# A decode step on one Trainium2 core: V's products at 256 columns, one quarter of wo in uneven loads, x in one load

## The chip, the cores and the metric

The kernel runs on one core of one Trainium2 chip. A core has a matrix engine (TensorE, PE in the profile; its weight loads are PEld), a vector engine (DVE), a scalar engine (ACT), a general engine (POOL), and SyncE (SP), which here only issues DMAs. Sixteen DMA engines bring data from HBM into SBUF, the on-chip memory of 128 partitions; PE writes its sums to PSUM. The metric is the device time of one execution in microseconds, the median of several runs. Times in the profile and in the trace are counted from the start of the profiled span.

## The reference

For 8 sequences of one new token each, the input x (8 x 512) is layer-normed to xn. Two branches use xn, and their product is added to x:

```python
q = (xn @ wq)                       # 32 heads of 128; 8 KV heads, so 4 query heads share one
k, v = last 1024 rows of the caches # of 4096, for each sequence and KV head
p = softmax(q k^T / sqrt(128))
s = (p v) @ wo                      # 4096 -> 512
g = silu((gelu(xn @ w_gate) * (xn @ w_up)) @ w_down)   # 512 -> 1792 -> 512
out = x + s * g
```

All inputs are bf16. Read in a run: K and V windows of 8 sequences (16 MB each in units of 1,048,576 bytes), wq and wo (4 MB each), and the three feed-forward matrices (1.75 MB each), 47.46 million bytes in all.

## The kernel before, in words

The order of the work is written out by hand: each engine runs its instructions in the order of the program, and waits are put in between by the framework, for data and for buffers.

All large loads go through SP's queue, in this order: the first quarter of wo (`wo_first`, line 106), wq (line 109), K of sequence 0, K of 1, V of 0 (line 84, each cache block in two loads of 1 MB, one for each half `g` of the KV heads), then K and V of the following sequences alternating, w_gate and w_up (line 438), w_down (line 441), and the other three quarters of wo (line 451). The buffers are a ring of eight slots of 2 MB. The compiled program has eight completion semaphores for all loads together, x's included; a load is issued when the load eight places before it has landed and when its buffer is free. A load of 128 partitions consists of one packet for each contiguous row: 8 KB for K, V and a quarter of wo, 32 KB for wq, 14 KB for the feed-forward matrices. The last quarter of wo comes in three pieces (5, 2 and 1 KB for each partition), so that products can start on the first of them. x comes through ACT's queue, in five loads of 2, 2, 2, 1 and 1 rows (line 79).

Ahead of the loop over the sequences: DVE takes the mean and variance of x (line 145), ACT the root (line 149), DVE scales (`xhat`, line 152), and ACT loads its table for the exponential by a small activation into a tile of its own (`warm`, line 162). PE multiplies xn with wq (line 261), and the queries are laid out block-diagonally (`qbd`).

For each sequence `b` the functions below run in an order that overlaps sequences:

- `turn_k` transposes one half of K on DVE (line 249), `scores` makes the products with the queries (line 311).
- `softmax` takes the maximum (lines 321 to 328), and ACT forms the exponentials and, through its accumulator, their sums over the row (line 333). The sums go to a column of the tile `sums`.
- `turn_p` transposes the probabilities on DVE (line 344). `values` multiplies them with V (line 355): for each of the two halves `g`, 32 products of 128 columns, in four column groups of PE that accumulate side by side.
- `keep_o` copies the result to SBUF on ACT (line 368); `gather` adds the four groups up on PE with a selection matrix, first the 128 values (line 376), and then the sums (line 380), once for each `g`. `regroup` divides by the sums and turns the result for wo, once for four sequences.

After the loop come the products with w_gate and w_up (line 465), the gelu, those with w_down (line 494), and at last the 128 products with wo (line 513) in the order of its quarters. Two DVE steps (lines 521 and 523) and one output DMA (line 525) end the kernel.

Of the kernel before, what the change touches and what calls it, by code (L numbers as in the profile page):

```python
# [7 lines left out]
ACT = mybir.ActivationFunctionType  # L8
# [3 lines left out]
FP32 = mybir.dt.float32  # L12
# [9 lines left out]
def kernel(  # L22
# [13 lines left out]
    nc = tc.nc  # L36

    B, Sq, D = A_x.shape
    Hkv, Sk, Dh = A_k_cache.shape[1], A_k_cache.shape[2], A_k_cache.shape[3]
# [6 lines left out]
    P = nc.NUM_PARTITIONS  # L46
    NK = D // P
    HG = 4
    NG = Hkv // HG
    C = W * HG // P  # L50
# [7 lines left out]
    keep = ctx.enter_context(tc.tile_pool(name="keep", bufs=1))  # L58
    two = ctx.enter_context(tc.tile_pool(name="two", bufs=2))
# [7 lines left out]
    def slot(name):  # L67
        i = taken[0] % N_SLOTS
        taken[0] += 1
        if i >= 2:  # L70
            return ring.tile([P, 2 * ROW], BF16, name=name, tag="slot")
        if not late:
            late.append(ctx.enter_context(tc.tile_pool(name="late", bufs=2)))
        return late[0].tile([P, 2 * ROW], BF16, name=name, tag="slot")


    x_sb = keep.tile([B, D], BF16, name="x_sb")
    for r, z in ((0, 2), (2, 4), (4, 6), (6, 7), (7, 8)):
        nc.scalar.dma_start(out=x_sb[r:z], in_=A_x.flatten_outer_dims()[r:z])  # L79

    def load_cache(cache, b, name):
# [10 lines left out]
    k_sb, v_sb = {}, {}  # L92
# [4 lines left out]
    def load_v(b):  # L97
# [3 lines left out]
    wo_src = [  # L101
        A_wo[u * 1024 : (u + 1) * 1024, :].rearrange("(p j) d -> p j d", j=8)
        for u in range(NU)
    ]
# [14 lines left out]
        out=ident,  # L119
        in_=ident,  # L120
# [13 lines left out]
        out=xpad,  # L134
        in_=xpad,
# [8 lines left out]
    stats = keep.tile([B, nc.vector.BN_STATS_DIM], FP32, name="stats")  # L144
# [3 lines left out]
    rstd = keep.tile([B, 1], FP32, name="rstd")  # L148
# [4 lines left out]
        out=xhat,  # L153
# [4 lines left out]
        op1=ALU.mult,  # L158
    )
    x_res = keep.tile([P, DT], FP32, name="x_res")  # L160
    warm = keep.tile([B, 1], FP32, name="warm")
    nc.scalar.activation(out=warm, in_=rstd, func=ACT.Exp)  # L162
    with tc.tile_pool(name="ps_x", bufs=1, space=PSUM) as ps_x:
        xnT_ps = ps_x.tile([P, NK, B], BF16, name="xnT_ps")
        xv = xhat.rearrange("b (p k) -> b k p", k=NK)
# [5 lines left out]
        for t in range(4):  # L171
# [4 lines left out]
                start=True,  # L176
                stop=True,
# [12 lines left out]
        out=hv,  # L190
        in_=hv,
# [7 lines left out]
        out=neg_st,  # L199
        in_=neg_st,  # L200
# [8 lines left out]
        out=neg_mv,  # L209
        in_=neg_mv,  # L210
# [9 lines left out]
    sel = consts.tile([P, NG, Hq], FP32, name="sel")  # L220
    nc.vector.memset(sel, 0.0)
    for g in range(NG):
        nc.vector.tensor_reduce(
            out=sel[:, g, g * qd : (g + 1) * qd],
            in_=ident.rearrange("p (t g h) -> p g h t", t=4, g=NG)[:, g],
# [5 lines left out]
        out=own, in_=ident.rearrange("p (i e) -> p e i", e=8), axis=AX.X, op=ALU.add  # L231
    )
    pick = consts.tile([P, 4 * NU], BF16, name="pick")
    with nc.allow_low_precision(reason="sums of zeros and a single one"):
        nc.vector.tensor_reduce(
            out=pick, in_=ident.rearrange("p (a e) -> p a e", e=8), axis=AX.X, op=ALU.add
# [20 lines left out]
    with tc.tile_pool(name="ps_q", bufs=1, space=PSUM) as ps_q:  # L257
        q_ps = [ps_q.tile([P, 512], FP32, name=f"q_ps{i}") for i in range(8)]
        for k in range(NK):
            for i in range(8):  # L260
# [4 lines left out]
                    start=(k == 0),  # L265
                    stop=(k == NK - 1),
                )
        for half in range(2):
            for i in range(4 * half, 4 * half + 4):
                e = nc.vector.tensor_copy if i % 4 == 3 else nc.scalar.copy  # L270
# [7 lines left out]
    for j in range(4):  # L278
        sl = slice(32 * j, 32 * j + 32)
        for m in range(2):  # L280
            for g in range(NG):
                e = nc.scalar.copy if (4 * j + 2 * m + g) % 3 == 2 else nc.vector.tensor_copy
# [3 lines left out]


    pT, S, P_sb, O_ps = {}, {}, {}, {}
    sums = keep.tile([P, B], FP32, name="sums")

    actx = ExitStack()
    ps_s = actx.enter_context(tc.tile_pool(name="ps_s", bufs=2, space=PSUM))
# [26 lines left out]
    def softmax(b):  # L319
        mx = two.tile([P, 1], FP32, name="mx")  # L320
        nc.vector.tensor_reduce(  # L321
            out=mx, in_=S[b].rearrange("p a c -> p (a c)"), axis=AX.X, op=ALU.max
        )

        m2 = two.tile([64, 1], FP32, name="m2")
        nc.vector.tensor_tensor(out=m2, in0=mx[0:64, :], in1=mx[64:128, :], op=ALU.max)
        m1 = two.tile([32, 1], FP32, name="m1")
        nc.vector.tensor_tensor(out=m1, in0=m2[0:32, :], in1=m2[32:64, :], op=ALU.max)  # L328
        nb = two.tile([P, 1], FP32, name="nb")
        for j in range(4):  # L330
            nc.scalar.mul(nb[32 * j : 32 * j + 32, :], m1, -inv)  # L331
        P_sb[b] = two.tile([P, C // 2, 32, 2], BF16, name="P_sb")
        nc.scalar.activation(  # L333
            out=P_sb[b].rearrange("p c i w -> p c w i"),
            in_=S[b].rearrange("p a (c w i) -> p (a c) w i", w=2, i=32),
            func=ACT.Exp,
            bias=nb,
            scale=inv,
            accum_out=sums[:, b : b + 1],
        )  # L340

    def turn_p(b):
        pT[b] = two.tile([P, C // 2, Hq, 2], BF16, name="pT")
        nc.vector.transpose(  # L344
            out=pT[b].rearrange("p c h w -> p (c h w)").bitcast(I32),
            in_=P_sb[b].rearrange("p c i w -> p (c i w)").bitcast(I32),
        )

    def values(b):
        O_ps[b] = ps_o.tile([P, NG, Dh], FP32, name="O_ps")  # L350
        for g in range(NG):
            vv = v_sb[b][:, g].rearrange("p (c d) -> p c d", d=Dh)
            for c in range(C):
                t = c % 4
                nc.tensor.matmul(  # L355
                    O_ps[b][32 * t : 32 * t + 32, g, :],
                    pT[b][:, c // 2, :, c % 2],
                    vv[:, c, :],
                    start=(c < 4),
                    stop=(c >= C - 4),  # L360
                )

    o_ps = {}
    O_sb = {}

    def keep_o(b):
        O_sb[b] = two.tile([P, NG, Dh], FP32, name="O_sb")
        nc.scalar.copy(out=O_sb[b], in_=O_ps[b])  # L368

    def gather(b):  # L370
        q = b % 4
        if q == 0:
            o_ps[b // 4] = ps_g.tile([P, Dh + 1], FP32, name="o_ps")
        o = o_ps[b // 4][32 * q : 32 * q + 32, :]
        for g in range(NG):
            nc.tensor.matmul(  # L376
                o[:, 0:Dh], sel[:, g, :], O_sb[b][:, g, :], start=(g == 0), stop=(g == NG - 1)
            )
        for g in range(NG):
            nc.tensor.matmul(  # L380
                o[:, Dh : Dh + 1],
                sel[:, g, :],
                sums[:, b : b + 1],
                start=(g == 0),
                stop=(g == NG - 1),
            )

    def regroup(q):

# [24 lines left out]
    for b in range(B):  # L414
        if b + 2 < B:
            load_k(b + 2)
        if b + 1 < B:
            load_v(b + 1)
            turn_k(b + 1, 0)
        softmax(b)  # L420
        if b + 1 < B:
            scores(b + 1, 0)
        if b >= 1:
            gather(b - 1)
        if b + 1 < B:
            turn_k(b + 1, 1)
            scores(b + 1, 1)
        turn_p(b)
        values(b)
        keep_o(b)  # L430
        if b == 4:
            regroup(0)
# [10 lines left out]
    for u in range(1, NU):  # L443
        if u % 2 == 1:
            pair = slot("wo_sb").rearrange("p (v j d) -> p v j d", v=2, d=D)
        t = pair[:, (u - 1) % 2]
        pieces = [(0, 8)]
        if u == NU - 1:
            pieces = [(0, 5), (5, 7), (7, 8)]
        for a, z in pieces:  # L450
            nc.sync.dma_start(out=t[:, a:z, :], in_=wo_src[u][:, a:z, :])
        wo.append(t)

    gather(B - 1)
    regroup(1)
    actx.close()
# [4 lines left out]
    for n, ws in (("z_ps", wgu[0]), ("u_ps", wgu[1])):  # L461
        ps = ps_f.tile([P, FT], FP32, name=n)
        for k in range(NK):
            for t in range(4):
# [4 lines left out]
                    start=(k == 0),  # L469
                    stop=(k == NK - 1),  # L470
# [6 lines left out]
        out=z2, in0=z2, scalar1=0.044715, scalar2=1.0, op0=ALU.mult, op1=ALU.add  # L477
# [11 lines left out]
        out=hT.rearrange("p j b -> p (j b)"), in_=h_bf.rearrange("p (y j) -> p j y", j=NJ)  # L489
    )  # L490
    f_ps = ps_f.tile([P, DT], FP32, name="f_ps")
    for j in range(NJ):
        for t in range(4):
# [4 lines left out]
                start=(j == 0),  # L498
                stop=(j == NJ - 1),
# [4 lines left out]
        out=g_sb, in0=g_sb, scalar1=0.5, scalar2=0.5, op0=ALU.mult, op1=ALU.add  # L504
# [5 lines left out]
    for u in range(NU):  # L510
        for j in range(8):
            for t in range(4):
# [4 lines left out]
                    start=(u == 0 and j == 0),  # L517
                    stop=(u == NU - 1 and j == 7),
# [7 lines left out]
        out=out_f.rearrange("b (t d) -> t b d", t=4), in_=out_sb[0 : P : RB, :]  # L526
# [31 lines left out]
```

## Time and profile before

| | |
|---|---|
| median of 3 runs | 120.89 us (120.85 to 120.97) |
| the profiled execution | 120.88 us |
| its span | 119.0 us |
| busy PE / DVE / ACT | 72.0 / 75.8 / 31.4 us |
| PE records (matmuls; as many weight loads) | 992 |
| DMA moved | 47.60 MB, mean 400 GB/s |
| V products (line 355) | 512, 9.5 us |
| gather of the values (line 376) | 32 records, 5.4 us |
| O_sb copies on ACT (line 368) | 8, 372 ns each |

The strip of slices gives, for 40 equal parts of the span, the busy share of each engine in tenths, the share of the DMA engines and what they moved. The list of DMA queues tells whose packets they were: q1 is SP's, q10 is ACT's, q8 and q14 carry instructions to the engines. The chain of work that ended last is followed back from the last instruction, at each step to what released it. A group is all instructions of one line, engine and shape, with the idle time of the engine ahead of them and what ended it. Busy time by stretch gives the same for chosen parts of the span, with the PE clock that was granted, the DMA share and GB/s at the end of a row. The trace holds besides, for each DMA packet, start, length, size and queue.

### The profile page before, as it was taken

The page shows a single profiled execution, that of the slowest core. Times are in us where ns is not written, and L with a number is a line of the kernel's source. Part 1 is how long each engine was busy: PE and PEld are TensorE (multiplying, and loading weights), DVE is VectorE, ACT ScalarE, POOL GpSimd, SP SyncE. Part 2 cuts the span into 40 slices and gives each one's busy share as a digit, 9 for nine tenths or more (in the row PEclk, how much of TensorE's full clock was granted, in tenths as well). Part 3 has the DMA queues.
Part 4 walks back from the last instruction along what each step waited for, and adds up shares of the span by engine and source line. Part 5 has one row for each costly group of instructions (what it writes and reads, how often), then busy time and mean ns, then how long its engine had stood idle before and what let it go on. Part 6 is the DMA issues. An engine that isn't in the chain of part 4 may idle for free.

```text
span 119.0 us, 2306 instructions
## 1 busy us (share of the span) xinstructions
PE 72.0 (61%) x992; PEld 37.5 (32%) x992; DVE 75.8 (64%) x101; ACT 31.4 (26%) x75; POOL 3.2 (3%) x10
## 2 busy tenths in 40 slices
PE   0000079941599596979964875698399264844650
PEld 0000033410133253545532434244135253414530
DVE  1000487999999999999957995971994224165100
ACT  1300230096202417170531421151070800120000
POOL 2000052000000000000000000000000000000000
PEclk9999999999679999999999999689859955578595
DMA  2998999999999999999999999999999999999930
GB/s 72 458 507 375 391 421 424 435 427 427 427 430 419 424 435 419 427 430 416 432 424 424 421 430 427 419 435 421 427 424 427 440 434 430 419 431 416 415 138 3
DMA packets 6109, 47.60 MB, mean 400 GB/s; under 512 B 716, under 2 KB 852, under 8 KB 1108
## 3 DMA queue, kind: packets, MB, share of 16 engines
q1 hardware_dynamic: 6084, 47.46, 94.6%
q8 instruction: 7, 0.11, 0.3%
q14 instruction: 2, 0.02, 0.0%
q10 hardware_dynamic: 16, 0.01, 0.0%
HBM read 47.46 MB, written 0.01 MB: 399 GB/s over the span
## 4 chain that ended last, share of the span: by engine, by line
DMA 61%; DVE 15%; PE 15%; ACT 3%; issue 2%; ACTq 1%; DVEq 0%
DMA wo_sb<-in_A_wo_dram 19%; DMA k_sb<-in_A_k_cache_dram 17%; DMA v_sb<-in_A_v_cache_dram 17%; DMA x_sb<-in_A_x_dram 9%; PE q_ps L261 7%; PE S_ps L311 6%; DVE kT L249 6%; DVE qbd L284 2%; DVE mx L321 2%; DVE q_both L274 1%; ACT P_sb L333 1%; ACTq L79 1%; ACT L162 1%; DVE q_both L271 1%; PE O_ps L355 1%
## 5 line engine op out<-in xcount | busy, mean ns | idle before, releaser
L311 PE MATMUL S_ps<-kT,qbd 128*128 128x512 bf16 x128 | 34.8, 420 | 15.4 <-DVE kT L249 12.0
L249 DVE STREAM_TRANSPOSE kT<-k_sb 128x2048 int32<-128x2048 int32 x16 | 36.6, 2289 | 5.0 <-DMA k_sb<-in_A_k_cache_dram 4.9
L311 PEld LDWEIGHTS <-qbd 128*128 128x128 bf16 x128 | 13.0, 103 | 33.3 <-issue 18.0
L331 ACT ACTIVATE nb<-m 32x1 f32<-32x1 f32 x32 | 6.4, 201 | 22.9 <-DVE m L328 22.6
L333 ACT ACTIVATE P_sb<-S_ps,nb 128x1024 bf16<-128x1024 f32 x8 | 11.1, 1391 | 0.3
L355 PE MATMUL O_ps<-v_sb,pT 128*32 128x128 bf16 x512 | 9.5, 231 | 2.6 <-DVE pT L344 2.6
L321 DVE TENSOR_REDUCE mx<-S_ps 128x1 f32<-128x1024 f32 x8 | 9.6, 1195 | 1.7 <-PE S_ps L311 1.6
L355 PEld LDWEIGHTS <-pT 128*32 128x32 bf16 x512 | 8.0, 103 | 5.6 <-issue 3.0
L261 PE MATMUL q_ps<-wq_sb,xnR 128*128 128x512 bf16 x32 | 9.2, 460 | 0.5 <-ACT x_res L179 0.5
L167 PE MATMUL xnT_ps<-ident,xhat 8*128 8x8 bf16 x4 | 0.3, 174 | 15.0 <-DVE xhat L152 15.0
L368 ACT COPY O_sb<-O_ps 128x256 f32<-128x256 f32 x8 | 3.0, 372 | 23.7 <-PE O_ps L355 23.7
L145 DVE BATCH_NORM_STATS2 stats<-x_sb 8x6 f32<-8x512 bf16 x1 | 0.7, 683 | 11.8 <-DMA x_sb<-in_A_x_dram 11.8
L344 DVE STREAM_TRANSPOSE pT<-P_sb 128x512 int32<-128x512 int32 x8 | 5.7, 711 | 3.4 <-ACT P_sb L333 3.3
L376 PE MATMUL o_ps<-O_sb,sel 128*32 128x128 f32 x32 | 5.4, 296 | 1.0 <-ACT O_sb L368 1.0
L300 PE MATMUL S_ps<-neg_mv,neg_st 128*128 128x512 bf16 x16 | 4.8, 381 | 1.9 <-DVE q_both L271 1.9
L261 PEld LDWEIGHTS <-xnR 128*128 128x128 bf16 x32 | 3.6, 114 | 5.8 <-issue 3.0
L271 ACT CAST q_both<-q_ps 128x512 bf16<-128x512 f32 x6 | 3.0, 613 | 7.9 <-PE q_ps L261 7.9
L167 PEld LDWEIGHTS <-xhat 8*128 8x128 bf16 x4 | 0.2, 114 | 15.0 <-DVE xhat L152 15.0
L376 PEld LDWEIGHTS o_ps<-O_sb,sel 128*32 128x32 f32 x32 | 3.0, 115 | 4.7 <-issue 3.2
L513 PE MATMUL s_ps<-wo_sb,oT 128*32 128x128 bf16 x96 | 2.7, 252 | 2.2 <-DMA wo_sb<-in_A_wo_dram 2.2
L252 DVE MEMSET qbd<- 128x4096 uint32 x1 | 3.5, 3472 | 0.8 <-issue 0.8
L513 PEld LDWEIGHTS <-oT 128*32 128x32 bf16 x128 | 3.0, 123 | 2.8 <-issue 2.6
(65 smaller groups left out, 51.1 us busy)
## 6 DMA issues: line engine op xcount, KB each, us to landing
k_sb<-in_A_k_cache_dram SPq DMA_DIRECT2D x16, 1024.0 KB, 19.7
v_sb<-in_A_v_cache_dram SPq DMA_DIRECT2D x16, 1024.0 KB, 19.8
wq_sb<-in_A_wq_dram SPq DMA_DIRECT2D x1, 4096.0 KB, 14.2
wo_sb<-in_A_wo_dram SPq DMA_DIRECT2D x2, 1024.0 KB
wgu_sb<-in_B_w_gate_dram SPq DMA_DIRECT2D x1, 1792.0 KB
wgu_sb<-in_B_w_up_dram SPq DMA_DIRECT2D x1, 1792.0 KB
wd_sb<-in_B_w_down_dram SPq DMA_DIRECT2D x1, 1792.0 KB, 25.1
wo_first<-in_A_wo_dram SPq DMA_DIRECT2D x1, 1024.0 KB, 4.8
```

Of the source, the lines that this page charges most:

```text
L249: nc.vector.transpose(out=t.bitcast(I32), in_=k_sb[b][:, g].bitcast(I32))
L261: nc.tensor.matmul(q_ps[i], xnR[:, k, :, :].rearrange("p j b -> p (j b)"), wq_sb[k][:, i * 512 : (i + 1) * 512], start=(k == 0), stop=(k = ...
L271: e(out=q_bf[:, i * 512 : (i + 1) * 512], in_=q_ps[i])
L300: nc.tensor.matmul(S[b][:, half, :], neg_st.rearrange("p j h -> p (j h)"), neg_mv.rearrange("p a n -> p (a n)"), start=True, stop=False,)
L311: nc.tensor.matmul(S[b][:, half, :], qbd[:, m, b, w, g, :], kv[:, half * 16 : (half + 1) * 16, m, :, w], start=False, stop=(g == NG - 1 an ...
L321: nc.vector.tensor_reduce(out=mx, in_=S[b].rearrange("p a c -> p (a c)"), axis=AX.X, op=ALU.max)
L331: nc.scalar.mul(nb[32 * j : 32 * j + 32, :], m1, -inv)
L333: nc.scalar.activation(out=P_sb[b].rearrange("p c i w -> p c w i"), in_=S[b].rearrange("p a (c w i) -> p (a c) w i", w=2, i=32), func=ACT.Exp,
L344: nc.vector.transpose(out=pT[b].rearrange("p c h w -> p (c h w)").bitcast(I32), in_=P_sb[b].rearrange("p c i w -> p (c i w)").bitcast(I32),)
L355: nc.tensor.matmul(O_ps[b][32 * t : 32 * t + 32, g, :], pT[b][:, c // 2, :, c % 2], vv[:, c, :], start=(c < 4), stop=(c >= C - 4),)
L376: nc.tensor.matmul(o[:, 0:Dh], sel[:, g, :], O_sb[b][:, g, :], start=(g == 0), stop=(g == NG - 1))
L513: nc.tensor.matmul(s_ps[32 * t : 32 * t + 32, :], oT[:, j, u, :], wo[u][:, j, t * DT : (t + 1) * DT], start=(u == 0 and j == 0), stop=(u = ...
```

## The change

Four things are edited.

1. `values` makes one product for both halves `g`: 256 columns in place of 128, 32 products for a sequence in place of 64.
2. The sums lie in a 129th column of `O_sb`: the accumulator of the exponential writes it for the first half, and an added ACT copy of 128x1 repeats it for the second. `gather` then multiplies 129 columns at once, and its separate products for the sums go. `O_sb` is allocated in `softmax`, and `keep_o` copies into its first 128 columns. The tiles `sums` and `warm` go; the exponential ahead of the loop writes into `stats`.
3. The second quarter of wo comes in five loads: 6 KB of each row for all 128 partitions, and the last 2 KB of each row for partitions 0 to 95, 96 to 120, 121 to 125, and 126 to 127.
4. x comes in one load of eight rows.

```diff
-    for r, z in ((0, 2), (2, 4), (4, 6), (6, 7), (7, 8)):
+    for r, z in ((0, 8),):
         nc.scalar.dma_start(out=x_sb[r:z], in_=A_x.flatten_outer_dims()[r:z])
...
-    warm = keep.tile([B, 1], FP32, name="warm")
-    nc.scalar.activation(out=warm, in_=rstd, func=ACT.Exp)
+    nc.scalar.activation(out=stats[:, 0:1], in_=rstd, func=ACT.Exp)
...
-    sums = keep.tile([P, B], FP32, name="sums")
...
+        O_sb[b] = two.tile([P, NG, Dh + 1], FP32, name="O_sb")
         nc.scalar.activation(
...
-            accum_out=sums[:, b : b + 1],
-        )
+            accum_out=O_sb[b][:, 0, Dh : Dh + 1],
+        )
+        nc.scalar.copy(out=O_sb[b][:, 1, Dh : Dh + 1], in_=O_sb[b][:, 0, Dh : Dh + 1])
...
-        for g in range(NG):
-            vv = v_sb[b][:, g].rearrange("p (c d) -> p c d", d=Dh)
-            for c in range(C):
-                t = c % 4
-                nc.tensor.matmul(
-                    O_ps[b][32 * t : 32 * t + 32, g, :],
-                    pT[b][:, c // 2, :, c % 2],
-                    vv[:, c, :],
-                    start=(c < 4),
-                    stop=(c >= C - 4),
-                )
+        vv = v_sb[b].rearrange("p g (c d) -> p c g d", d=Dh)
+        for c in range(C):
+            t = c % 4
+            nc.tensor.matmul(
+                O_ps[b][32 * t : 32 * t + 32, :, :],
+                pT[b][:, c // 2, :, c % 2],
+                vv[:, c, :, :],
+                start=(c < 4),
+                stop=(c >= C - 4),
+            )
...
-        O_sb[b] = two.tile([P, NG, Dh], FP32, name="O_sb")
-        nc.scalar.copy(out=O_sb[b], in_=O_ps[b])
+        nc.scalar.copy(out=O_sb[b][:, :, 0:Dh], in_=O_ps[b])
...
-            nc.tensor.matmul(
-                o[:, 0:Dh], sel[:, g, :], O_sb[b][:, g, :], start=(g == 0), stop=(g == NG - 1)
-            )
-        for g in range(NG):
-            nc.tensor.matmul(
-                o[:, Dh : Dh + 1],
-                sel[:, g, :],
-                sums[:, b : b + 1],
-                start=(g == 0),
-                stop=(g == NG - 1),
-            )
+            nc.tensor.matmul(o, sel[:, g, :], O_sb[b][:, g, :], start=(g == 0), stop=(g == NG - 1))
...
-        pieces = [(0, 8)]
+        pieces = [(0, 8, 0, P)]
+        if u == 1:
+            pieces = [(0, 6, 0, P)] + [(6, 8, p, e) for p, e in ((0, 96), (96, 121), (121, 126), (126, P))]
         if u == NU - 1:
-            pieces = [(0, 5), (5, 7), (7, 8)]
-        for a, z in pieces:
-            nc.sync.dma_start(out=t[:, a:z, :], in_=wo_src[u][:, a:z, :])
+            pieces = [(0, 5, 0, P), (5, 7, 0, P), (7, 8, 0, P)]
+        for a, z, p, e in pieces:
+            nc.sync.dma_start(out=t[p:e, a:z, :], in_=wo_src[u][p:e, a:z, :])
```

## The prediction

> **What bounds the kernel now.** I read the strip of 40 slices and the DMA queues first, then the chain of work that ended last, then busy time by stretch, the groups, and the waits of SP's queue.
>
> ```profile
> DMA  2998999999999999999999999999999999999930
> GB/s 72 458 507 375 391 421 424 435 427 427 427 430 419 424 435 419 427 430 416 432 424 424 421 430 427 419 435 421 427 424 427 440 434 430 419 431 416 415 138 3
> ...
> q1 hardware_dynamic: 6084, 47.46, 94.6%
> q8 instruction: 7, 0.11, 0.3%
> q14 instruction: 2, 0.02, 0.0%
> q10 hardware_dynamic: 16, 0.01, 0.0%
> ```
>
> From the second slice to the 38th the 16 DMA engines are full at some 425 GB/s. 47.46 MB at that pace is 112 us of the 119.0. The kernel is one stream of loads on SP's queue (q1). What else the engines carry is small: seven blocks of instructions on q8 (0.11 MB / 7 = 16 KB each), two of 8 KB on q14, and x on q10.
>
> ```profile
> 2.25 10.72 DMA x_sb<-in_A_x_dram
> ...
> 92.84 22.23 DMA wo_sb<-in_A_wo_dram
> 115.07 0.04 issue
> 115.11 0.59 PE s_ps L513 x12
> 115.71 0.02 issue
> 115.73 0.30 DVE y L521
> 116.03 0.02 issue
> 116.06 0.29 DVE out_sb L523
> ```
>
> In order of time the chain starts with 10.7 us for x and ends with wo's last piece, landed at 115.07. What follows (twelve products, two DVE steps, the output's DMA) takes 119.02 - 115.07 = 3.95 us, and the change leaves it alone.
>
> ```profile
> 60.00:75.00 15.00, 9.93 (x172) 5.47 (x172) 11.32 (x12) 3.46 (x10) 0.00 (x0) 1.00 1.01 426
> ...
> 112.60:115.10 2.50, 1.09 (x52) 0.80 (x52) 0.00 (x0) 0.00 (x0) 0.00 (x0) 1.00 0.65 245
> ```
>
> The last three figures of a stretch are the granted PE clock, the DMA share and GB/s. The share is 1.01 in mid-kernel and 0.65 in the last 2.5 us: there each engine idles 0.35 x 2.5 = 0.88 us on average. The 16 engines do not finish together, and the slowest sets 115.07.
>
> The trace's packet records say which. A packet has a start, a length, a size and a queue, but no engine; an engine shows as a string of packets, each starting within some 10 ns of the end of the last. The 16 strings end so: seven without a q8 or q14 packet at 113.26 to 113.82; two with one 8 KB block at 114.28 and 114.39; seven with one 16 KB block at 114.67, 114.82, 114.84, 114.92, 114.92, 114.95 and 115.07. A 16 KB block itself takes 0.88 to 0.96 us, and the packet behind it comes some 0.46 us late, so it costs its engine about 1.4 us. The mean of the ends is 114.22: perfect balance would be worth 0.85 us and no more. The only two strings with more than one x packet carry no 16 KB block.
>
> **The change part by part.** The profiled execution took 120.88 us (span 119.02, so 1.86 outside it); the median shown is 120.89. The sum is made against 120.88.
>
> *V's products and the sums.* Per batch 64 products of 128 columns become 32 of 256; a batch takes 1.08 us of PE (1.90 at half clock). Columns stay the same, so the after lies between 0.54 (time by instruction) and 1.08 (by column). The four matmul records of the sums' gather go (0.26 us a batch). ACT gains eight copies of 128x1; the nearest row, the accumulator read of the same shape, is 0.18 us. ACT waits 2.9 us for the V products before each O_sb copy, which covers it. All of it counts nothing: the stream does not wait for compute in these stretches, and at the end PE stands idle for loads,
>
> ```profile
> L513 PE MATMUL s_ps<-wo_sb,oT 128*32 128x128 bf16 x96 | 2.7, 252 | 2.2 <-DMA wo_sb<-in_A_wo_dram 2.2
> ```
>
> 1.06 us of that 2.2 ahead of wo's third quarter. If this cover went, the last chain's saving (about 0.4 us at half clock) would be felt; what is late next is the loads in any case.
>
> *Fewer instruction blocks.* At the seven blocks' times 306, 504, 834, 1031, 1211, 1548 and 1869 records of PE and its weight loads had run: one per 260. After, 2 x (992 - 256 - 32) = 1408 records remain, so five blocks (306, 566, ... 1347). Two engines get 1.4 us back, but only the slowest counts. If the first five stay where they are, the last end is still 115.07 (the fifth block's string): value 0. If the five were any of the seven strings, the best case without the 115.07 one ends at 114.95, and base strings differ by 0.37 us (113.26 to 113.63 without x): bounds -0.4 and +0.2 as blocks meet other strings. I take 0, the row as it is.
>
> *wo's second quarter.* Before, an engine moves eight packets of 8 KB and a completion mark: paces are 306 ns per 8 KB, 193 per 5 KB, 80 per 2 KB, 5 per mark, so 2453 ns. 6 KB lies between at 231. An engine outside the odd loads now moves 8 x 231 + 6 x 80 + 2 x 5 = 2338: -0.12 us. Those that take the 32 odd rows (25, 5, 2) get the difference. No row shows where a load of 25 goes. x's loads of two rows sent two packets at the same instant on two strings, those of one row one packet: few rows, few engines. Bounds: spread evenly over all 16 (two each), the pieces cost +0.06 in added packets and marks; on two engines only (16 each), -0.12 on fourteen and about +1.2 on two. By the nearest row I take few engines: some five, with six extra packets each, at 8 x 231 + 12 x 80 + 4 x 5 = 2828: +0.38, which ends a string without a block at about 114.0. The slowest falls by 0.12.
>
> [...]
>
> *Queue order.* SP issues a load only when the load eight before it has landed,
>
> ```profile
> SPq L525 <- DMA wgu_sb<-in_B_w_gate_dram: 3.9, 1, 3.9
> SPq L84 <- DMA x_sb<-in_A_x_dram: 5.1, 3, 1.9
> ```
>
> as the output's wait for w_gate, eight loads ahead, shows. Three more issues in wo's tail and a fourth make that rule reach back over fewer bytes: the last piece now waits for the 6 KB part of the second quarter, landed about 109.5. From issue to first packet wo_first took 1.65 us, so it is ready at 111.2; the earliest string needs it at about 112.8. Cost 0, with 1.6 us to spare; the issue itself is 0.33 us, four more are 1.3 us on an SP that waits anyway.
>
> *x in one load.* ACT issues one DMA in place of five (0.24 to 0.54 us each). The DVE's 11.8 us wait ahead of L145 goes: x lands at about 2 to 5 us instead of 13.0 (its first packets came at 1.73, its second load's behind wo_first at 5.22). The q products then start when wq has landed (its last packet ends at 15.10) and not at 16.03: 0.6 to 0.9 us earlier on the compute side. On the stream side it counts nothing, since the DMA share is 1.01 in the stretches from 15 us on and SP's lead is some 20 us. For the engines: the two that took 5 and 3 packets of x save four and two of 52 ns, six others gain one. At the very start the two x strings finished wo_first at 5.21 us, the others at 4.82 to 5.22; bounds for eight engines with x in front +0.2 and -0.2, taken 0.
>
> Sum: 120.88 - 0.12 = 120.76.
>
> **The rivals.**
> *Faster.* The five blocks avoid the slowest strings, or the start is better by 0.2: last end down 0.3 to 0.4 in all. For: seven strings lie within 0.4 us, two lose their block. Against: the 115.07 string's block is the fifth and stays. Time 120.88 - 0.36 = 120.52.
> *Slower: a block meets the odd rows.* If one of the five blocks falls on an engine that carries the odd rows, its end of 114.82 to 115.07 moves by +0.38 (with all three loads on it +0.46): 115.2 to 115.5. It decides as soon as one does; more make no difference. For: nothing in the trace numbers the engines. Against: the two x strings, which by x's packets take the small loads first, have no 16 KB block. Time about 120.88 + 0.32 = 121.2.
> *The pieces do not do what they should.* The 96-row load reaches 96 of 128 partitions, and engines may meet at their entrances to SBUF as they never do in loads of 128. If six 2 KB packets (0.48 us) ran a quarter slower, that would give the 0.12 back: 120.88. Against: no row of before shows such a load or such a meeting, and the strings are spread over 1.8 us, so that neighbours are seldom in the same piece. [...]
> *The tail of loads starves.* If latency to the last piece were over 1.6 us more, the end moves by the excess; 121.3. Against: 20 us of lead.
> *x pulls everything.* By the chain's face the 0.6 to 0.9 us of earlier q products move the end: 120.1. Against: the full stream in between.
>
> **How the numbers follow.** A difference of 0.2% (0.24 us) is about what a measurement of this kernel can tell from no change. The forecast, 120.76: 0.31; the pieces' rival, 120.88: 0.08. Faster, 120.52: 0.28; x: 0.05. Slower by a block: 0.26; starving: 0.02. So faster 0.33, same 0.39, slower 0.28. The range takes in the faster case's bound (-0.45) and the slower one's up to +0.42: 120.43 to 121.3. The forecast's own range is 120.6 to 121.0.
>
> **What would show it.** Five q8 blocks in place of seven; V's group with x256; DVE's wait ahead of L145 down to 2 to 5 us; the chain's start without x, its end still wo_sb then 3.95 us. Right: the last landing at 114.9 to 115.0, a share in the last 2.5 us above 0.65. Wrong if the last landing is at 115.2 or later with one or two strings far behind (a block met the odd rows), if SP's queue issues the last piece after 111 (starving), or if the landing is before 114.7 (blocks or start).

## The result, and the profile after

The changed kernel is slower: 121.83 us (median of 18 runs, 121.47 to 122.04) against 120.97 us for the kernel before on the same chips, a ratio of 1.0062 with a 95% interval of 1.0049 to 1.0074. The forecast was no change (120.76 us), with a range up to 121.3 us.

The page of the changed kernel, strip of 40 slices and DMA queues:

```profile
DMA  2998999999999999999999999999999999999930
GB/s 79 470 491 360 396 437 426 426 423 429 434 426 423 418 434 426 423 426 423 429 423 426 429 423 431 429 418 423 434 429 430 444 430 421 425 409 316 396 114 3
DMA packets 6263, 47.57 MB, mean 396 GB/s; under 512 B 744, under 2 KB 880, under 8 KB 1392
...
q8 instruction: 5, 0.08, 0.2%
```

Seven instruction blocks have become five, as predicted. But the 37th slice (108 to 111 us) moves 316 GB/s, where the 37th of the kernel before moved 416, and the engines are as busy there as elsewhere. The share is full and the flow is not; below this is called the *dip*. The same in figures, busy time by stretch of the kernel before, and then of the changed one (the last three columns are the granted PE clock, the DMA share and GB/s):

```profile
108.00:111.50 3.50, 2.70 (x116) 2.70 (x120) 1.26 (x3) 0.28 (x1) 0.00 (x0) 0.67 1.01 427
```

```profile
108.00:111.50 3.50, 2.77 (x112) 2.59 (x112) 0.99 (x3) 0.28 (x1) 0.00 (x0) 0.63 1.04 323
...
112.60:115.10 2.50, 0.63 (x32) 0.48 (x32) 0.00 (x0) 0.00 (x0) 0.00 (x0) 1.00 0.84 324
```

In 3.5 us some 104 GB/s are missing, 0.36 MB, which at 427 GB/s is 0.85 us of the whole stream. In the last 2.5 us before the old end the share is 0.84 where it was 0.65, not because the engines finish together but because all are late: the 16 completions of wo's last piece run from 114.38 to 116.37 us, before from 113.61 to 115.40. The end of the chain shows where it went:

```profile
83.16 25.09 DMA wd_sb<-in_B_w_down_dram
108.25 0.02 issue
108.27 7.78 DMA wo_sb<-in_A_wo_dram
116.05 0.04 issue
116.10 0.64 PE s_ps L503 x11
116.73 0.02 issue
116.76 0.30 DVE y L511
117.06 0.02 issue
117.08 0.29 DVE out_sb L513
```

The last landing in the chain is at 116.05 us in place of 115.07, 0.98 us later; the tail behind it is 3.99 us in place of 3.95. The span grew from 119.02 to 120.04 us. So nearly the whole loss lies in the stream of loads, and in one place of it. (It is the completion of wo's 2 KB piece, the one before the last, which the trace records some 0.35 us behind the piece's last packet; the table below takes the end of the last packet of wo, 115.06 and 116.02 us in these two traces.)

The packet records tell which packets were slow. An 8 KB packet takes 309 ns nearly everywhere. In the changed kernel 74 of the 128 packets of wo's third quarter (8 KB) took over 345 ns, up to 548; 26 of the second quarter's 6 KB packets took 295 to 493 instead of about 234, and the uneven 2 KB ones up to 178 instead of 84. I added up, over all packets that start after 106 us, what each took beyond the usual time of its size, and divided by 16: 0.93 us for each engine (in all 14.9: 8.5 in 8 KB packets, 3.0 in 6 KB, 3.3 in 2 KB). In the kernel before the same sum is 0.03 us. Below it is called *lengthening*.

### The profile page after: what moved, and what is told of

It reads as the page before. It is cut to its first block, busy times and chain, and to the rows that moved or that the text cites. A ratio compares the mean times of both kernels' runs of the same rounds, so it can differ in the third digit from the quotient of the medians.

```text
span 120.0 us, 1737 instructions
## 1 busy us (share of the span) xinstructions
PE 71.3 (59%) x704; PEld 33.6 (28%) x704; DVE 76.0 (63%) x101; ACT 32.9 (27%) x83; POOL 3.2 (3%) x10
## 4 chain that ended last, share of the span: by engine, by line
DMA 88%; PE 8%; DVE 0%; issue 0%; SPq 0%
DMA k_sb<-in_A_k_cache_dram 48%; DMA wd_sb<-in_B_w_down_dram 21%; DMA wq_sb<-in_A_wq_dram 12%; PE q_ps L260 8%; DMA wo_sb<-in_A_wo_dram 6%; PE s_ps L503 1%; SPq L106 0%; DVE y L511 0%; DVE out_sb L513 0%; SPq L84 0%; SPq L429 0%
## 5 line engine op out<-in xcount | busy, mean ns | idle before, releaser
L354 PE MATMUL O_ps<-v_sb,pT 128*32 128x256 bf16 x256 | 9.3, 292 | 2.7 <-DVE pT L344 2.7
L354 PEld LDWEIGHTS <-pT 128*32 128x32 bf16 x256 | 6.5, 102 | 6.3 <-issue 3.0
L374 PE MATMUL o_ps<-O_sb,sel 128*32 128x129 f32 x32 | 5.5, 297 | 1.0 <-ACT O_sb L366 1.0
L270 DVE CAST q_both<-q_ps 128x512 bf16<-128x512 f32 x2 | 1.3, 671 | 4.0 <-ACT q_both L270 4.0
L283 DVE COPY qbd<-q_both 32x256 bf16<-32x256 bf16 x11 | 3.4, 358 | 0.0
```

The lines of the kernel that those rows point to most:

```text
L270: e(out=q_bf[:, i * 512 : (i + 1) * 512], in_=q_ps[i])
L354: nc.tensor.matmul(O_ps[b][32 * t : 32 * t + 32, :, :], pT[b][:, c // 2, :, c % 2], vv[:, c, :, :], start=(c < 4), stop=(c >= C - 4),)
L374: nc.tensor.matmul(o, sel[:, g, :], O_sb[b][:, g, :], start=(g == 0), stop=(g == NG - 1))
```

## The experiments

Two kinds of question stood open: which of the parts does it, and by what. All runs are held against the kernel before on the same chip (120.96 to 121.00 us). Times are medians; "closing" is the time from the output's last packet to the end of the span.

| run | loads | time, us | ratio, 95% | lengthening, us | last landing | closing |
|---|---|---|---|---|---|---|
| before | 47 | 120.97 | | 0.03 | 115.06 | 1.16 |
| after | 47 | 121.83 | 1.0049 to 1.0074 | 0.93 | 116.02 | 1.16 |
| uneven loads alone | 51 | 122.17 | 1.0080 to 1.0126 | 1.04 | 116.02 | 1.41 |
| after without them | 43 | 121.33 | 1.0013 to 1.0034 | 0.03 | 114.97 | 1.42 |
| 2 KB in one load | 44 | 121.32 | 1.0018 to 1.0041 | 0.03 | 115.14 | 1.35 |
| 96 and 32 rows | 45 | 122.39 | 1.0093 to 1.0138 | 1.02 | 116.42 | 1.29 |
| V alone | 47 | 121.01 | 0.9986 to 1.0009 | 0.03 | 115.10 | 1.16 |
| five even loads | 47 | 121.21 | 0.9999 to 1.0025 | 0.03 | 115.43 | 1.17 |
| uneven, 1 KB | 47 | 121.39 | 1.0021 to 1.0053 | 0.24 | 115.18 | 1.16 |
| 64 and 64 rows | 45 | 122.65 | 1.0102 to 1.0147 | 1.26 | 116.50 | 1.28 |
| x alone | 43 | 121.30 | 0.9996 to 1.0037 | 0.03 | 115.16 | 1.42 |
| rows read in another order | 44 | 122.39 | 1.0048 to 1.0152 | 1.12 | 116.31 | 1.35 |
| even and odd partitions | 45 | 121.38 | 1.0001 to 1.0043 | 0.03 | 115.07 | 1.28 |
| written by halves | 45 | 122.43 | 1.0107 to 1.0145 | 1.17 | 116.20 | 1.28 |
| read by halves | 45 | 121.35 | 1.0019 to 1.0040 | 0.03 | 115.08 | 1.28 |

"Loads" counts the DMAs ahead of the output's.

### Which part: the uneven loads alone, and the change without them

```diff
# uneven loads alone: the kernel before, with
+        if u == 1:
+            pieces = [(0, 6, 0, P)] + [(6, 8, p, e) for p, e in ((0, 96), (96, 121), (121, 126), (126, P))]
# the change without them: the changed kernel, with
-        if u == 1:
-            pieces = ...
```

> The kernel before with only the uneven loads of wo's second quarter. Changed kernel against before: +0.86 us in the medians; in its trace the last landing moved from 115.07 to 116.05 and the stream fell from 427 to 250 to 360 GB/s between 108 and 111.5 us, as the odd loads ran. Theory (engines meet at the same partitions of SBUF while a load's rows are not laid out as those of a 128-row load): the dip is here as well, 121.6 to 122.2 us, some more than the changed kernel if two more instruction blocks count (+0.0 to +0.2). Rival A (2 KB packets and additional loads are the cost, not where they write): the same time, so this run does not tell it apart. Rival B (the dip comes from x or from V's products, which only moved other work into this stretch): no dip, 120.8 to 121.0 us.

> The changed kernel with wo's second quarter in one load again (V's products at 256, x in one load stay). Theory: no dip, share 1.01 and 425 GB/s up to 112 us, five instruction blocks, last landing 114.8 to 115.1; 120.7 to 121.0 us. Rival B: dip and 121.6 us or more.

The uneven loads alone took 122.17 us (+1.03%), with a lengthening of 1.04 us: the theory held, and rival B fell. The change without them has no dip, but it was expected at 120.7 to 121.0 and took 121.33, though its last loads landed at 114.97, 0.09 us earlier than before. Busy time by stretch, that run:

```profile
108.00:111.50 3.50, 3.39 (x120) 3.22 (x121) 0.51 (x2) 0.28 (x1) 0.00 (x0) 0.50 1.02 432
```

The stream is whole again, and yet its profiled span is 119.31 us, 0.29 us longer than before. Most of that lies behind the output's last packet: closing is 1.42 us instead of 1.16. That is a second effect, taken up below ("The count of loads").

### Small packets, or where they are written

```diff
-  for p, e in ((0, 96), (96, 121), (121, 126), (126, P))]
+  for p, e in ((0, P),)]                # 2 KB in one load
+  for p, e in ((0, 96), (96, P))]       # 96 and 32 rows
```

> The changed kernel with the last 2 KB of the second quarter's rows in one load of all 128 partitions (6 KB, then 2 KB). Theory of meeting at partitions: every engine writes to the same partitions as in all other loads, so no dip; eight more packets and a mark per engine cost 0.06 us; 120.75 to 121.1 us. Rival A (small packets): as many 2 KB packets as in the changed kernel, dip of the same size, 121.6 us or more.

> The changed kernel with the 2 KB parts in loads of 96 and 32 partitions. By the packet marks of the changed kernel, 96 rows went to 16 engines with six each; 32 should go to 16 with two each, so all engines carry the same bytes and no engine gets extra rows, but rows lie on other engines than in a load of 128. Theory of meeting at partitions: a dip, perhaps shorter, 121.2 to 121.9 us. Rival C (the cost is the extra rows on the first five engines, which then stand in the way of the others): no dip, 120.75 to 121.1 us.

The two runs move the same bytes in packets of the same size, one load more in the second. Their stretches (2 KB in one load, then 96 and 32 rows):

```profile
108.00:111.50 3.50, 2.98 (x116) 2.98 (x120) 0.98 (x3) 0.28 (x1) 0.00 (x0) 0.50 1.04 432
```

```profile
108.00:111.50 3.50, 3.22 (x112) 2.93 (x112) 0.64 (x3) 0.28 (x1) 0.00 (x0) 0.50 1.06 318
```

432 GB/s against 318, lengthening 0.03 against 1.02 us. So the size of packets is not the cause (rival A falls), nor are extra rows on a few engines (rival C falls: with 96 and 32 every engine should have eight rows; the page of that run has 32 more marks than the kernel before, so each of its two loads did run on 16 engines). The time of 2 KB in one load, 121.32, was above its expected 120.75 to 121.1 by the closing again (1.35 us). The dip with 96 and 32 was not shorter than the changed kernel's, as I had guessed, and 122.39 lies above the expected 121.9.

### V's products alone, five even loads, half the bytes

```diff
# V alone: the changed kernel with x in five loads and wo's second quarter in one
# five even loads
-            pieces = [(0, 6, 0, P)] + [(6, 8, p, e) for ...]
+            pieces = [(a, z, 0, P) for a, z in ((0, 4), (4, 5), (5, 6), (6, 7), (7, 8))]
# uneven, 1 KB
-            pieces = [(0, 6, 0, P)] + [(6, 8, p, e) for ...]
+            pieces = [(0, 7, 0, P)] + [(7, 8, p, e) for ...]
```

> The kernel before with V's products at 256 columns and the sums in O_sb alone: x in five loads, wo's second quarter in one. 47 loads stand ahead of the output, as in the kernel before and in the changed one. The runs without pieces or with an even 2 KB part (43 and 44 loads) ended 0.20 to 0.27 us later after the output's last packet: SP's closing waits run over the eight completion semaphores in turn at some 0.065 us each, and with 47 loads the output's own is the last of them, with 43 the fourth from the end. Theory (the end depends on the count of loads modulo eight, and V's products are worth nothing): last landing 114.8 to 115.1, output's last packet to end of span 1.1 us, 120.8 to 121.1 us. Rival (V's products or the instruction blocks themselves make the end later): 121.2 us or more.

> The changed kernel with wo's second quarter in five loads all of 128 partitions (4 KB and four times 1 KB of each row): 47 loads as in the changed kernel, the output's semaphore last, only no load with rows off their usual engines. Packets and marks cost about 0.17 us per engine more than one load. Theory (the uneven rows alone make the changed kernel slower): no dip between 108 and 112 us, last landing 115.0 to 115.3, 120.9 to 121.2 us. Rival (additional loads, short packets or later issues by the eight-load rule): as the changed kernel, 121.6 to 122.0 us.

> The changed kernel with 7 KB of the second quarter's rows for all partitions and the last 1 KB (instead of 2 KB) in loads of 96, 25, 5 and 2: half the bytes in uneven rows, same number of loads. Theory (each uneven byte costs while it is written): the loss between 107.5 and 112 us about halves, last landing 115.4 to 115.7, 121.3 to 121.5 us. Rival (a fixed cost of such loads, or of engines set apart from one another, whatever their size): 121.7 to 122.0 us.

V's products alone are worth nothing: 121.01 us, ratio 0.9998, five blocks, last landing 115.10. The group itself shows that the time was nearer the bound by column: half as many products, and 8.8 us in place of 9.5. First the kernel before, then V alone:

```profile
L355 PE MATMUL O_ps<-v_sb,pT 128*32 128x128 bf16 x512 | 9.5, 231 | 2.6 <-DVE pT L344 2.6
```

```profile
L354 PE MATMUL O_ps<-v_sb,pT 128*32 128x256 bf16 x256 | 8.8, 280 | 2.7 <-DVE pT L344 2.7
```

Five even loads in place of the uneven ones, with the same count of loads, gave 121.21 us, 0.62 us less than the changed kernel, and a lengthening of 0.03 us, that of the kernel before. This is the plain control: same V, same x, same number of loads, same closing; the added loads are even and of 1 KB a row. Of the 0.86 us that the changed kernel lost, 0.6 or more are the unevenness. The run lies 0.01 us above its expected range, and its last landing, 115.43, is 0.37 us later than before, where added packets and marks had been put at 0.17; the rest was not followed.

Half the uneven bytes cost a quarter: lengthening 0.24 us instead of 0.93, 121.39 us. The time is as expected, but the last landing, 115.18, is ahead of the expected 115.4 to 115.7, and by its lengthening neither statement holds, that each byte costs the same or that the cost is fixed. Why it grows faster than the bytes is open.

### Which side: halves, every second partition, reading and writing

```diff
# 64 and 64 rows
+  for p, e in ((0, 64), (64, P))]
# the next three replace the 2 KB loads; p runs over 0 and 1 in all but the first
# rows read in another order (one load of 128)
+  out=t[:, 6:8, :], in_=A_wo[1024:2048, :].rearrange("(b a j) d -> a b j d", b=8, j=8)[:, :, 6:8, :]
# even and odd partitions
+  out=t[p:P:2, 6:8, :], in_=wo_src[u][p:P:2, 6:8, :]
# written by halves
+  out=t[64 * p : 64 * p + 64, 6:8, :], in_=wo_src[u][p:P:2, 6:8, :]
# read by halves
+  out=t[p:P:2, 6:8, :], in_=wo_src[u][64 * p : 64 * p + 64, 6:8, :]
```

> The changed kernel with the 2 KB parts in two loads of 64 partitions (45 loads, so 0.13 us of closing waits; to be held against the run of 96 and 32 rows with the same count, 122.39 us). Every engine carries four rows of each. [...] Rival (only a count that is not a power of two, or rows that begin off a multiple of four, disturbs): no dip, 121.0 to 121.3 us.

> The changed kernel with the last 2 KB of the second quarter in one load of all 128 partitions, whose rows are read from wo in another order (partition 8a+b gets row a+16b), so that this part of wo lies on the wrong partitions and the output differs; loads, bytes and packets are those of the run with an even 2 KB part (121.32 us; the same 44 loads). Theory (the disturbance is on the side of SBUF, where the rows are written): no dip, at most 0.1 us of lengthened packets per engine, 121.1 to 121.5 us. Rival (the disturbance is in HBM, from reading rows that other engines usually read): a dip as with 96 and 32 rows, 121.9 us or more. A dip would also come if such a load's rows were dealt to the engines in another way than those of a plain load of 128, so a dip would leave the side open.

> The changed kernel with the 2 KB parts in two loads of 64 partitions each, the even and the odd partitions, in place of the lower and the upper half (45 loads, as the run with 64 and 64, 122.65 us, with 1.26 us of lengthened packets per engine, and the run with 96 and 32, 122.39 us and 1.02 us). Each load reaches all of SBUF, four rows per engine. [...] Rival (any row written away from the engine's usual partitions costs the same): 1.0 us or more per engine, 122.2 us or more.

64 and 64 rows were the worst, 122.65 us and 1.26 us of lengthening, so it does not take a crooked number. Every second partition instead, also 64 and 64 rows, has none: 0.03 us, and 121.38 us. That is against the rival (1.0 us or more) only if these rows were written away from the engines' usual partitions, and a packet record does not name its engine. Rows read in another order showed a dip (1.12 us), which the theory of SBUF had not expected; as its expectation says, this run leaves the side open, since the load may also have been dealt to the engines in another way. The last pair changes one side at a time, with two loads of 64 throughout.

> The changed kernel with the 2 KB parts in two loads of 64 rows: read from the even and the odd rows of wo's second quarter, as in the run with even and odd partitions (121.38 us, 0.03 us of lengthened packets per engine), but written to the lower and the upper 64 partitions, as in the run with 64 and 64 (122.65 us, 1.26 us). The rows of this part lie on the wrong partitions, so the output differs. 45 loads. [...] Rival (HBM: engines disturb one another when they read rows that are not their usual ones): at most 0.1 us per engine, 121.1 to 121.5 us.

> The other pairing: read from the lower and the upper 64 rows of wo's second quarter, written to the even and the odd partitions; the output differs for the same reason. 45 loads. Theory (SBUF): at most 0.1 us of lengthened packets per engine, 121.1 to 121.5 us. Rival (HBM): 0.9 us or more per engine, 122.1 us or more. If both runs show a part, both sides take part.

Busy time by stretch, written by halves:

```profile
108.00:111.50 3.50, 3.28 (x112) 2.93 (x112) 0.52 (x2) 0.28 (x1) 0.00 (x0) 0.50 1.07 304
```

and read by halves:

```profile
108.00:111.50 3.50, 3.38 (x120) 3.20 (x121) 0.51 (x2) 0.28 (x1) 0.00 (x0) 0.50 1.03 427
```

The four runs form a square. Lengthening per engine:

| | read even and odd rows | read lower and upper rows |
|---|---|---|
| written to even and odd partitions | 0.03 | 0.03 |
| written to lower and upper half | 1.17 | 1.26 |

In these four runs, what counts is the partitions that a load writes, and not the rows of HBM that it reads. How the partitions come to count is argued, not shown. One account, a guess of mine, is crowding: engines that write one block of the partitions (64, 96, 25) get in one another's way. The last pair fits it, 304 GB/s when the halves are written and 427 when they are read, but no trace shows where the engines would meet.

The run with rows read in another order does not fit so simply. Its load wrote all 128 partitions, and it lengthened packets by 1.12 us all the same, so reaching every partition is not enough. Either its rows were dealt to the engines in another way, or this order of reading costs something by itself; no run tells which. A second account fits the whole table if the dealing went that way: what costs is an engine that writes to partitions that another engine fills in a whole load. No run holds it apart from crowding, as it is not known which engine took which rows. The runs show the side, for loads of 64, and the pattern.

### The count of loads: x alone

```diff
-    for r, z in ((0, 2), (2, 4), (4, 6), (6, 7), (7, 8)):
+    for r, z in ((0, 8),):
```

> The kernel before with x in one load alone: 43 loads ahead of the output. Theory of the closing waits (the output's semaphore is then the fourth of eight from the end instead of the last): output's last packet to end of span 1.42 us instead of 1.16, x landed at about 2 to 5 us, last landing as before within 0.1, 121.15 to 121.35 us. Rival (x early takes part of the way, and shows once V's products stay as they are): 120.3 to 120.9 us. Rival (no effect of either): 120.85 to 121.05 us.

Closing is 1.42 us and the median 121.30, so the theory's numbers hold; the ratio's interval (0.9996 to 1.0037) takes in no change, and the closing in the trace is the surer reading. x landed at 2.85 us instead of 12.67. In the queue's waits it is this line, first of the kernel before and then with x alone (us in total, times, longest):

```profile
SPq L553 <- DMA out_dram<-out_sb: 0.8, 1, 0.8
```

```profile
SPq L553 <- DMA out_dram<-out_sb: 1.0, 1, 1.0
```

At the end SP goes through the completion semaphores in six steps, each 0.06 to 0.07 us behind the one before where nothing has to be waited for; some steps take two semaphores. The trace names the semaphore of the output's DMA and of each step. With 47 loads the output's stands in the sixth step, and all others have been gone through while the output was in flight. With 43 or 51 it stands in the second, and four more steps come behind the landing: 4 x 0.065 = 0.26. With 44 it is the third, with 45 the fourth: the place follows the count of loads modulo eight. The table bears it out at each count: 1.16 (47), 1.28 and 1.29 (45), 1.35 (44), 1.41 and 1.42 (51 and 43).

This also says why the parts do not add up. x alone costs +0.16% and takes four loads away, the uneven loads alone cost +1.03% and bring four; together the count is 47 again, both closings of 0.26 us are gone, and the sum is +0.62%, not +1.19%. The two closings are 0.52 of the 0.69 us between those figures; another 0.11 is the larger lengthening of the uneven loads alone (1.04 against 0.93).

## Why the prediction was wrong

- *wo's second quarter* is the step that failed. It reckoned the uneven loads by the number of packets on each engine, -0.12 us for those outside, and took the pace of a packet as given, for these loads and for those around them. The runs show +0.93 us for each engine from lengthened packets; 8.5 of the 14.9 engine-us fell on the third quarter, a load that was not edited. The engines were counted right, all 16 for the 96 rows and some five for the odd ones: in the trace of the changed kernel the four loads have 16, 5, 5 and 2 completions on their semaphores, and the page counts 744 packets under 512 B, before 716, the 28 more being their marks.
- The rival *the pieces do not do what they should* pointed to the right side, the partitions that a load writes (1.17 and 1.26 us against 0.03 in the square), and mis-sized the loss. That engines meet at entrances to SBUF, as it has it, no run shows. The rival let six 2 KB packets run a quarter slower (0.12 us) and gave it a chance of 0.08. The term measured 0.93. Its argument against, that the strings are 1.8 us apart and neighbours seldom in the same piece, did not hold: over half of the lengthening (8.5 of 14.9 engine-us) fell on packets of whole loads, so a packet need not be in a piece to be slowed.
- *The forecast for the block rival* (a block meets the odd rows, 121.2) gave the right sign by another cause. Five even loads, with the same five blocks, end at 121.21, so blocks need not enter. The sign that the prediction set for it, a last landing at 115.2 or later, came (116.05), but not with one or two strings far behind: the share in the last 2.5 us rose from 0.65 to 0.84. Whether one did meet the odd rows in the changed kernel stays open, since the strings cannot be followed through the dip.
- *V's products and the sums* counted nothing, and are worth nothing (0.9986 to 1.0009).
- *Instruction blocks*: five, as worked out, and with five blocks and the second quarter in one load the last landing is at 114.97 and 115.10 (115.06 before), so the value 0 was right.
- *x in one load* counted nothing on the stream: right. Its last packet ended at 2.44 us in the changed kernel, as predicted (2 to 5), and the naive reading of the chain (9% for x) gains nothing. But the step did not see that four loads fewer move the output's semaphore; in this change that was hidden by the four loads added.
- *Queue order*: right in its cost of 0. The last piece was issued by 111.3 us at the latest (SP's last issue of wo ended at 85.60 + 25.65), which may be past the 111 that was named as the sign of starving; but the DMA share stays at 1.0 and above until 113.5 us, and the first packet of the last piece started at 113.61, some 2.3 us after that issue, more than the 1.65 it was given. So nothing starved. (The 1.65 us from issue to first packet holds for most of wo_first's packets at the start; four of them came from 1.02 us on.)
- The tail of 3.95 us stayed (3.99).

## What to carry to other kernels

When loads fill the DMA engines, a full share with fewer GB/s is the sign to look for (here 1.04 with 323 GB/s, against 1.01 with 427): compare the two per stretch. Do not cut a load into blocks of partitions to shift work between engines while the stream is full, as the cuts made here lengthened packets by 0.24 to 1.26 us for each engine; cutting along the row with all 128 partitions, or taking every second partition, stayed at 0.03. All 128 partitions are no guarantee: read in another order, such a load cost 1.12. And where the end of a kernel waits for several semaphores in turn, count the DMAs: whether the last one's semaphore is in the last step was worth up to 0.26 us here, and it makes parts of a change look better or worse than they are.

## What the runs showed that I had not expected

- 256 KB of a 47 MB stream, written by blocks of partitions, lengthened packets by 14.9 to 20.1 engine-us; at their usual 84 ns the 128 uneven packets need 10.8. So others lose time too, 8.5 engine-us in the changed kernel's third quarter alone. With 1 KB it is 3.8. What makes it more than sharing stays open.
- The same cut into two loads of 64 lengthens nothing when each takes every second partition: 0.03 us, no more than a load of 128.
- SP's closing steps of 0.065 us; and that the number of loads decides how many of them lie behind the output's landing.
